# Smaller first loads at the head of a gated S5 + GELU-MLP kernel: first x slab alone, first weight slab in halves, one small load on another queue

## The chip, the cores and the metric

One core of a Trainium2 chip. The metric is the device time of one execution in microseconds (us). Runs repeat within about half a per cent for this kernel, so I give medians, ranges and the fastest runs, not only one time. "Ratio" is the mean time of one kernel's runs over the mean of the other's runs in the same rounds, so it is not quite the ratio of the medians that stand beside it.

## The reference, cut to what matters

Two branches over the same x (2048 tokens, 640 features), mixed by a gate:

```python
g = sigmoid((x * gate_w).sum(-1, keepdims=True))
a = S5(x)                      # x @ B_bar, a complex linear recurrence over time, @ C, + x * Dskip
b = gelu(x @ w1 + b1) @ w2 + b2        # w1: 640 x 1728
out = g * a + (1 - g) * b
```

Only the start of `x @ w1` matters here. The kernel contracts over 640 features in five steps of 128, called k=0 to k=4. For each step it needs a 128-feature slab of x, transposed, and a slab of W1 (128 x 1024, 256 KB).

## The kernel before: the parts that the change touches

The kernel gives each engine an ordered list of operations; priorities and assumed durations decide the order when the program is built, and semaphores carry the dependencies. In the profile's lines PE is TensorE, DVE VectorE, ACT ScalarE, POOL GpSimd and SP SyncE; SPq and ACTq are the queues from which these two issue loads, and a bank is one of the eight parts PS[0] to PS[7] of the memory that TensorE writes. For the first 512 tokens, slabs 0 and 1 of x are loaded plainly and transposed on TensorE; slabs 2 to 4 are loaded by transposing DMAs. All these loads are issued by SyncE, one after the other:

```python
KN = 2
load("xna", "sp", "l_xna", xn[0][:, :, 0:KN * 128], x2[0:512, 0:KN * 128]..., ["xna"], 0, ...)
w1load(0, "sp", 1)                       # W1 slab 0, 256 KB
w1load(1, "sp", 1.3)
xtrans(0, range(KN, KN + 1), 1.6, 0.8)   # x slab 2, transposing DMA
w1load(2, "sp", 2)
xtrans(0, range(KN + 1, KD), 3, 1.3)     # x slabs 3 and 4, transposing DMA
w1load(3, "sp", 4)
w1load(4, "sp", 5)
# ... then W1's remaining columns, B_re, B_im, the other x tiles, W2, C ...
load("b1b", "pool", "l_b1b", rows[RT:RT + 1, :]..., ["b1b"], prio=-50, ...)   # a one-row bias, twice

for n in (512,) * 6 + (256,):            # warm-up matmuls on constants
    nc.tensor.matmul(PS[4][:, 0:n], one..., one..., start=True, stop=True)

# 8 transposes: x slab 0 in banks 7 and 6, x slab 1 in banks 5 and 7; DVE copies them to xT
# first W1 matmuls: for k in 0..4, for jf in 0..7:  PS[jf] += W1[k, jf].T @ xT[k]
#   (k=0, jf=0 and 1 come in halves of 256 columns; k=0, jf=7, whose bank the transposes use, comes after k=1, jf=6)
```

## Time and profile before

| | before |
|---|---|
| time, median of the first 3 runs | 213.44 us (212.94 to 213.54) |
| profiled run | 212.76 us, span 211.5 us |
| first W1 matmul | 4.57 us |
| first matmul of the next stage (B) | 18.66 us |

The two lines below are the page's part on the chain that ended last: what each step back from the last instruction waited for.

```profile
PE 98%; issue 0%; DVE 0%
PE ps L772 27%; PE ps L642 22%; PE ps L821 21%; PE ps L685 20%; PE ps L622 4%; PE ps L400 1%; PE ps L786 1%; PE ps L663 1%; PE ps L412 0%; DVE osb L855 0%; PE ps L431 0%
```

The chain is TensorE from end to end; no DMA stands in it. Only what delays TensorE counts.

The same chain in order of time, its first 11.5 us (start, length, what):

```profile
0.78 2.93 PE ps L400 x7
3.71 1.03 PE ps L412 x8
4.74 2.38 PE ps L622 x13
7.12 0.06 PE ps L431
7.17 4.32 PE ps L622 x20
```

L400 is the warm-up, L412 the transposes, L622 the first W1 matmuls, L431 a small transpose of bias and parameter rows. The timeline of SyncE, which issues the loads (start, length of the issue, what):

```profile
0.74 0.45 SPq L326 DMA_DIRECT2D xn<-in_A_x_dram  x1
1.25 0.96 SPq L326 DMA_DIRECT2D W1sb<-in_B_w_dram  x2
2.26 1.20 SPq L333 DMA_TRANSPOSE xT<-in_A_x_dram  x1
3.51 0.59 SPq L326 DMA_DIRECT2D W1sb<-in_B_w_dram  x1
4.15 1.28 SPq L333 DMA_TRANSPOSE xT<-in_A_x_dram  x1
5.47 2.10 SPq L326 DMA_DIRECT2D W1sb<-in_B_w_dram  x4
```

An issue costs SyncE 0.42 to 0.59 us for a plain load and 1.2 to 1.3 us for a transposing one. The fourth line is W1 slab 2, the first of the last four is slab 3.

### The profile page before, as it was taken

The numbers are of one execution on the slowest core, as the hardware profiler recorded it, in microseconds if no ns is written. First come the engines' busy times: TensorE is split into PE (matmuls) and PEld (weight loads), VectorE is DVE, ScalarE is ACT, GpSimd is POOL, SyncE is SP. The second block draws the span as 40 slices with busy tenths as digits, with TensorE's granted clock in tenths as the row PEclk, the third lists the DMA queues.
The fourth block names the chain that finished last, engine by engine and source line by source line (L and its number), as shares of the span: only waits on it lengthen the run. The fifth ranks groups of instructions, "written<-read, shape, count | busy, mean of one in ns | idle before, by whom it ended". The sixth has DMA issues, their size and how long they took to land.

```text
span 211.5 us, 3140 instructions
## 1 busy us (share of the span) xinstructions
PE 208.1 (98%) x1266; PEld 121.2 (57%) x1276; DVE 189.3 (90%) x264; ACT 111.3 (53%) x201; POOL 3.0 (1%) x11
## 2 busy tenths in 40 slices
PE   8999999999999999999999999999999999999996
PEld 4444444444567776444466777544446777767775
DVE  2599999999999999999999969899999999899444
ACT  2588556678904334556953333456792444723330
POOL 2000000000000010000000001000000000000000
PEclk9999999999999999999999999999999999999999
DMA  5999699999100013100000014100000000010011
GB/s 164 290 246 183 158 225 300 303 213 197 42 0 3 31 38 120 62 0 0 0 3 0 0 48 143 39 23 3 0 0 2 3 31 31 31 34 0 31 34 62
DMA packets 31350, 16.35 MB, mean 77 GB/s; under 512 B 23144, under 2 KB 30440, under 8 KB 31336
## 3 DMA queue, kind: packets, MB, share of 16 engines
q1 hardware_dynamic: 30960, 14.83, 28.5%
q0 software_dynamic: 320, 1.31, 2.0%
q8 instruction: 10, 0.16, 0.3%
q14 instruction: 4, 0.03, 0.1%
q10 hardware_dynamic: 56, 0.01, 0.0%
HBM read 7.63 MB, written 2.62 MB: 48 GB/s over the span
## 4 chain that ended last, share of the span: by engine, by line
PE 98%; issue 0%; DVE 0%
PE ps L772 27%; PE ps L642 22%; PE ps L821 21%; PE ps L685 20%; PE ps L622 4%; PE ps L400 1%; PE ps L786 1%; PE ps L663 1%; PE ps L412 0%; DVE osb L855 0%; PE ps L431 0%
## 5 line engine op out<-in xcount | busy, mean ns | idle before, releaser
L772 PE MATMUL ps<-W2sb,Gl 128*128 128x320 bf16 x416 | 59.2, 299 | 0.0
L772 PEld LDWEIGHTS ps<-W2sb,Gl 128*128 128x128 bf16 x416 | 40.4, 98 | 17.1 <-issue 1.1
L642 PE MATMUL ps<-xT,W1sb 128*128 128x512 bf16 x215 | 47.5, 379 | 0.3
L821 PE MATMUL ps<-CT,H 128*128 128x320 bf16 (+2 forms) x330 | 45.5, 295 | 0.0
L725 DVE TENSOR_TENSOR_SCAN W<-atab,V 128x1280 bf16<-128x1280 f32 x16 | 44.3, 2811 | 0.3
L685 PE MATMUL ps<-xT,BT 128*128 128x512 bf16 x196 | 43.1, 379 | 0.3 <-issue 0.2
L821 PEld LDWEIGHTS ps<-CT,H 128*128 128x128 bf16 x330 | 31.9, 98 | 11.7
L800 ACT ACTIVATE E<-ps,g1col 128x320 bf16<-128x320 f32 x32 | 16.3, 526 | 39.7 <-PE ps L772 25.6
L642 PEld LDWEIGHTS ps<-xT,W1sb 128*128 128x128 bf16 x220 | 21.5, 98 | 26.0
L649 ACT ACTIVATE Gl<-ps,cols 128x512 bf16<-128x512 f32 x44 | 29.6, 688 | 10.0 <-PE ps L642 10.0
L685 PEld LDWEIGHTS ps<-xT,BT 128*128 128x128 bf16 x200 | 19.4, 98 | 23.5 <-ACT Gt L671 0.4
L694 ACT ACTIVATE U<-ps 128x512 bf16<-128x512 f32 x40 | 23.8, 597 | 15.0 <-PE ps L685 14.9
L832 ACT ACTIVATE E<-ps,gcol 128x320 bf16<-128x320 f32 x30 | 15.8, 527 | 22.6 <-PE ps L821 22.6
L759 ACT ACTIVATE ps<-b2b 128x320 f32<-128x320 bf16 x32 | 14.1, 441 | 1.1
L481 DVE TENSOR_TENSOR osb<-xg,E 128x640 bf16<-128x640 bf16 x15 | 7.3, 487 | 7.9 <-ACT E L832 7.6
L842 DVE SCALAR_TENSOR_TENSOR xg<-xn,gcol,dsk 128x640 bf16<-128x640 bf16 x16 | 13.9, 882 | 0.4
L597 DVE SCALAR_TENSOR_TENSOR scr<-xn,gwb 128x640 bf16<-128x640 bf16 x16 | 13.2, 822 | 0.4
L481 DVE TENSOR_TENSOR H<-H,V 128x1280 bf16<-128x1280 bf16 x16 | 12.5, 821 | 0.3
L481 DVE TENSOR_TENSOR V<-V,W 128x1280 bf16<-128x1280 bf16 x16 | 12.5, 821 | 0.3
L481 DVE TENSOR_TENSOR V<-mr,U 128x2560 bf16<-128x2560 bf16 x8 | 11.9, 1488 | 0.2
L481 DVE TENSOR_TENSOR H<-c,W 128x2560 bf16<-128x2560 bf16 x8 | 11.9, 1488 | 0.2
L481 DVE TENSOR_TENSOR W<-mi,U 128x2560 bf16<-128x2560 bf16 x8 | 11.9, 1483 | 0.0
(80 smaller groups left out, 99.9 us busy)
## 6 DMA issues: line engine op xcount, KB each, us to landing
out_dram<-osb SPq DMA_DIRECT2D x15, 160.0 KB, 1.8
W2sb<-in_B_w_dram SPq DMA_DIRECT2D x1, 2080.0 KB, 8.9
W1sb<-in_B_w_dram SPq DMA_DIRECT2D x5, 256.0 KB, 3.9
xn<-in_A_x_dram POOLq DMA_DIRECT2D x2, 640.0 KB, 4.6
xn<-in_A_x_dram SPq DMA_DIRECT2D x1, 640.0 KB, 7.9
W1sb<-in_B_w_dram SPq DMA_DIRECT2D x1, 480.0 KB, 5.8
W1sb<-in_B_w_dram SPq DMA_DIRECT2D x1, 400.0 KB, 6.5
xn<-in_A_x_dram SPq DMA_DIRECT2D x1, 384.0 KB, 6.0
```

The lines of the kernel that those rows point to most:

```text
L481: return inc("dve", nc.vector.tensor_tensor(out=o, in0=a, in1=b, op=o_))
L642: t = nc.tensor.matmul(PS[bank][:, :], W1sb[:, k, jf * 128:(jf + 1) * 128], xT[q][:, k, :], start=(k == 0), stop=(k == KD - 1))
L649: return inc("act", nc.scalar.activation(Gl[q % 2][:, jf, :], PS[bank][:, :], ACT.Gelu_apprx_tanh, bias=b1col[:, jf:jf + 1]))
L685: t = nc.tensor.matmul(PS[bank][:, :], BT[:, ci, kd, k * 128:(k + 1) * 128], xT[q][:, kd, :], start=(kd == 0), stop=(kd == KD - 1))
L694: return inc("act", nc.scalar.activation(dst, src, ACT.Copy, scale=1.0 if ci == 0 else -1.0))
L725: t = inc("dve", nc.vector.tensor_tensor_scan(out=g[:, ci, :], data0=a, data1=v[:, ci, :], initial=0.0, op0=ALU.mult, op1=ALU.add))
L759: return inc("act", nc.scalar.activation(PS[bank][:, 0:HALF], b2b[:, cols], ACT.Copy))
L772: t = nc.tensor.matmul(PS[bank][:, 0:HALF], Gl[q % 2][:, jf, t4 * 128:(t4 + 1) * 128], W2sb[:, jf, cols], start=False, stop=False, skip_gr ...
L800: return inc("act", nc.scalar.activation(E1[c % NE][:, cols], PS[bank][:, 0:HALF], ACT.Copy, scale=g1col[:, c:c + 1]))
L821: t = nc.tensor.matmul(PS[bank][:, 0:n], H[b % NHB][:, ci, k, s * 128:(s + 1) * 128], CT[:, ci, k, cols], start=(i == 0), stop=(i == 2 * K ...
L832: return inc("act", nc.scalar.activation(E2[c % NE][:, cols], PS[bank][:, 0:HALF], ACT.Copy, scale=gcol[:, c:c + 1]))
L842: return inc("dve", nc.vector.scalar_tensor_tensor(out=xg[c % 2][:, :], in0=xn[q % 2][:, c % 4, :], scalar=gcol[:, c:c + 1], in1=dsk[:, :] ...
```

## The change

Its intent is to start the first W1 matmuls earlier: a smaller first x slab lands sooner, half of W1's first slab is enough for half of the k=0 matmuls, the second x slab is transposed while k=0 already runs, and one warm-up matmul becomes superfluous. The diff, cut to its core:

```diff
-        load("xna", "sp", "l_xna", xn[0][:, :, 0:KN * 128], ..., ["xna"], 0, dur=0.45, lat=2.0)
-        w1load(0, "sp", 1)
+        for k in range(KN):
+            load(f"xna{k}", "sp", f"l_xna{k}", xn[0][:, :, k * 128:(k + 1) * 128], ...,
+                 [("xna", k)], (0, 1.2)[k], dur=0.45, lat=(2.0, 2.6)[k])
+        for h in range(2):
+            f0, f1 = h * FW // 2, (h + 1) * FW // 2
+            load(f"w1_0{h}", "sp", f"l_w10{h}", W1sb[:, 0, f0:f1], B_w1[0:128, f0:f1], [("w1", 0, h)], prio=1 + 0.1 * h, lat=2.6)
 ...
-        load("b1b", "pool", "l_b1b", ..., ["b1b"], prio=-50, dur=1.0)
+        load("b1b", "act", "l_b1b", ..., ["b1b"], prio=-101, dur=1.2)
 ...
-            for n in (512,) * 6 + (256,):
+            for n in (512,) * 5 + (256,):
 ...
-  op(f"xt{i}", ..., ["xna", "ident"], ..., prio=(-990, -989, -988, 2.5)[i])
+  op(f"xt{i}", ..., [("xna", k), "ident"], ..., prio=(-990, -989, 6.4, 6.5)[i])
+        def f_fill():                      # one filler matmul of 192 columns
+            return inc("pe", nc.tensor.matmul(PS[4][:, 0:192], one..., one..., start=True, stop=True))
+        op("fill", "pe", 0.2, (), [("bank", 4)], f_fill, prio=-980)
 ... (dependencies follow the new names)
```

SyncE's order becomes: x slab 0, W1 slab 0 first half, second half, x slab 1, W1 slab 1, and then as before. That is two issues more ahead of everything else.

More of the change, by code (lines that the diff above doesn't have):

```diff
@@ L353, in bass_gated_mix__ssm_conv_s5__dense_activation_gelu__prompt_kernel @@
         KN = 2
-        load("xna", "sp", "l_xna", xn[0][:, :, 0:KN * 128], x2[0:512, 0:KN * 128].rearrange("(c p) d -> p c d", p=128), ["xna"], 0, dur=0.45, lat=2.0)
-        w1load(0, "sp", 1)
+        for k in range(KN):
+            load(f"xna{k}", "sp", f"l_xna{k}", xn[0][:, :, k * 128:(k + 1) * 128], x2[0:512, k * 128:(k + 1) * 128].rearrange("(c p) d -> p c d", p=128),
+                 [("xna", k)], (0, 1.2)[k], dur=0.45, lat=(2.0, 2.6)[k])
+        for h in range(2):
+            f0, f1 = h * FW // 2, (h + 1) * FW // 2
+            load(f"w1_0{h}", "sp", f"l_w10{h}", W1sb[:, 0, f0:f1], B_w1[0:128, f0:f1], [("w1", 0, h)], prio=1 + 0.1 * h, lat=2.6)
         w1load(1, "sp", 1.3)
@@ L376, in bass_gated_mix__ssm_conv_s5__dense_activation_gelu__prompt_kernel @@
             load(nm, "act", "l_" + nm, rows[r0:r0 + src.shape[0], :], src, [nm], prio=-100 + i, dur=0.4)
-        load("b1b", "pool", "l_b1b", rows[RT:RT + 1, :].rearrange("o (a p) -> o a p", a=2),
-             B_b1[nmain:F].rearrange("(o p) -> o p", o=1).unsqueeze(1).broadcast_to([1, 2, FL]), ["b1b"], prio=-50, dur=1.0)
+        load("b1b", "act", "l_b1b", rows[RT:RT + 1, :].rearrange("o (a p) -> o a p", a=2),
+             B_b1[nmain:F].rearrange("(o p) -> o p", o=1).unsqueeze(1).broadcast_to([1, 2, FL]), ["b1b"], prio=-101, dur=1.2)
         def f_iota():
@@ L413, in f_xt @@
                 return inc("pe", t)
-            op(f"xt{i}", "pe", 0.11 * (c1 - c0), ["xna", "ident"], [("bank", bank)], f_xt, prio=(-990, -989, -988, 2.5)[i])
+            op(f"xt{i}", "pe", 0.11 * (c1 - c0), [("xna", k), "ident"], [("bank", bank)], f_xt, prio=(-990, -989, 6.4, 6.5)[i])
             def f_xc(k=k, pt=pt, c0=c0, c1=c1):
@@ L420, in bass_gated_mix__ssm_conv_s5__dense_activation_gelu__prompt_kernel @@
             op(f"xc{i}", "dve", 0.42, [("bank", bank)], [("xT", 0, k, c0)], f_xc, prio=-2000 + i)
+        def f_fill():
+            return inc("pe", nc.tensor.matmul(PS[4][:, 0:192], one.broadcast_to([128, 128]), one.broadcast_to([128, 192]), start=True, stop=True))
+        op("fill", "pe", 0.2, (), [("bank", 4)], f_fill, prio=-980)
         XK0 = [[("xT", 0, k)] for k in range(KD)]
@@ L569, in bass_gated_mix__ssm_conv_s5__dense_activation_gelu__prompt_kernel @@
         load("xnb", "sp", "l_xnb", xn[0][:, :, KN * 128:D], x2[0:512, KN * 128:D].rearrange("(c p) d -> p c d", p=128),
-             [("xn", 0, 0), ("xn", 0, 1)], 32.4, dur=1.0, lat=6.0, reads=["xna"])
+             [("xn", 0, 0), ("xn", 0, 1)], 32.4, dur=1.0, lat=6.0, reads=[("xna", k) for k in range(KN)])
         load("w2a", "sp", "l_w2a", W2sb[:, 0:NF - 1, :], B_w2[0:nmain, :].rearrange("(j p) d -> p j d", p=128), ["w2a"], prio=33, lat=8.0)
@@ L623, in f_mm @@
                                                       start=(k == 0 and t0 == 0), stop=(k == KD - 1), skip_group_check=jf < 2))
-                op(f"m1_0_{jf}_{k}_{t0}", "pe", d_mm(t1 - t0), (XK0[k] if h is None else XK0[k][h:h + 1]) + [("w1", k)], [("bank", jf)],
+                op(f"m1_0_{jf}_{k}_{t0}", "pe", d_mm(t1 - t0), (XK0[k] if h is None else XK0[k][h:h + 1]) + ([("w1", k)] if k else [("w1", 0, jf // (NW // 2))]), [("bank", jf)],
                    f_mm, prio=pe_prio())
@@ L644, in f_mm @@
                     return inc("pe", t)
-                op(f"m1_{q}_{jf}", "pe", KD * d_mm(512), XT[q] + ([("w1", k) for k in range(KD)] if jf < NW else [("w1", "r", int(jf * 128 >= FM))]), [("bank", bank)], f_mm, prio=pe_prio())
+                op(f"m1_{q}_{jf}", "pe", KD * d_mm(512), XT[q] + ([("w1", k) for k in range(1, KD)] + [("w1", 0, 0), ("w1", 0, 1)] if jf < NW else [("w1", "r", int(jf * 128 >= FM))]), [("bank", bank)], f_mm, prio=pe_prio())
                 def f_ge(jf=jf, bank=bank):
```

## The prediction

> **What bounds the kernel now.** TensorE. The chain of work that ended last is 98% PE, and matmul starts are back to back (0.216 us per 128x512) from the first W1 matmul at 4.57 us to 209.5 us of the 211.5 us span. So only the head can change, and passes one to one to the end.
>
> The head before (timeline): warm-up matmuls 0.78 to 3.50 us at 0.427 us each, half speed; the x slabs (256 KB, issued 0.74) land 3.63; eight transposes 3.67 to 4.57 (six of them 0.107 us apart: still half clock); then W1. The granted clock is recorded as full from 4.39 us. The Trainium skill ("TensorE: Matmul & The Clock Gate", Part 1) says the clock is released after about 3.4 us of sustained activity in a free-running window; 0.78 to 4.39 agrees. Work started earlier runs at half clock until then.
>
> **What the change does.**
> - Removes one 512-wide warm-up (0.43 us), adds one 192-wide filler (0.16 us cold); four of eight transposes move behind the clock release (4 x 0.05 us saved).
> - The x slab of k=0 is 128 KB in 512 packets of 256 B instead of 512 B. Packet times in the trace are 27 ns at 512 B and 18 ns at 256 B, so about 0.29 us less over 16 engines (estimate): landing 3.35 to 3.5. First copy to xT then ends near 4.1 to 4.2 (0.72 us after the transpose starts, as before), first W1 matmul about 4.15 instead of 4.57. W1's first half (issue about 1.25) should land by about 4.0.
> - The second slab's transposes come in the middle of k=0, and W1 matmuls behind them need their copies: transpose to copied is 0.6 us, with only one 0.22 us matmul between. Estimate: 0.2 us stall before (k=0, jf=5) and k=1. Start of k=1: 6.1 to 6.2, against 6.09 before. Most of the head gain is given back.
> - SyncE issues two more DMAs ahead of the rest, 0.42 to 0.49 us each. Later loads are issued about 0.9 us later. From 4.5 us on the DMA engines were fully busy, so part is absorbed; estimate: landings 0.5 us later. Slack before (landing against first use): W1 slab 2 0.85 us, slab 3 0.36 us, slab 4 1.3 us, W1 remainder 0.95 us, B_re 1.5 us. Slab 3 becomes tight: a stall of 0 to 0.4 us at k=3 (about 9.9 us).
> - The bias row's load moves from POOL (landed 4.65) to ACT; its reader at 6.95 has slack. Nothing.
>
> **Sum.** Head about 0 (-0.3 to +0.2), slab stall about +0.1 (0 to +0.5): nearly zero. Predicted 213.4 us against 213.44, range 212.7 to 214.2. Faster by over 2%: 0.01; within 2%: 0.98; slower: 0.01.
>
> **What would show it.** Right: first x landing near 3.4; first W1 matmul near 4.1 to 4.2; first transposing load issued near 3.2 instead of 2.26; holes of 0.1 to 0.3 us in PE around 5.5 to 6.2; a wait on W1 slab 3 near 10 us; after 13 us all shifted alike, by under 0.5 us. Wrong: the x slab landing at 3.6 or later, or W1 slabs landing a full 0.9 us later (stall at k=3 of 0.5 us).
>
> **What would make it wrong.** The clock release coming a window later because PE idles between the shorter warm-up and the slab: up to +1.7 us. Or late issues wholly absorbed and the k=0 slab landing near 3.1: down to -0.5 us.

## The result, and the profile after

| | before | after |
|---|---|---|
| time, median of 6 runs | 213.19 us (212.88 to 213.89) | 213.81 us (213.73 to 214.12) |
| ratio | | 1.0028, 95% interval 1.0009 to 1.0048 |
| profiled run, span | 211.5 us | 212.4 us |
| first x load lands | 3.63 us | 3.02 us |
| first W1 matmul | 4.57 us | 4.21 us |
| first matmul of k=1 | 6.09 us | 6.68 us |
| W1 slabs 2, 3, 4 land | 7.24, 9.45, 10.21 us | 8.72, 10.51, 12.44 us |
| first matmul of the B stage | 18.66 us | 19.62 us |

Within 2%, and a little slower. From the first B matmul to the end the two profiled runs take 192.79 and 192.81 us: the whole difference lies in the head. The first W1 matmul does come 0.36 us earlier, and k=1 already starts 0.59 us later. The chain that ended last, on the page after:

```profile
PE 93%; SPq 3%; DMA 2%; issue 1%; DVE 0%
PE ps L781 27%; PE ps L651 22%; PE ps L830 20%; PE ps L694 20%; DMA W1sb<-in_B_w_dram 2%; SPq L326 2%; PE ps L795 1%; SPq L333 1%; PE ps L672 1%; PE ps L631 1%; DVE osb L864 0%
```

A DMA and SyncE are in the chain now. The 2% and the two SPq shares are small, but they replace all of TensorE's work of the first 12 us. In order of time, from 3.52 us on, up to 20 us (pieces under 0.1 us left out; before 3.52 us it is SyncE's issues):

```profile
3.52 1.20 SPq L333
4.77 0.58 SPq L326
5.40 1.25 SPq L333
6.69 0.58 SPq L326
7.31 5.13 DMA W1sb<-in_B_w_dram
12.49 1.90 PE ps L631 x8
14.39 5.40 PE ps L651 x25
```

Read it from the bottom: the k=4 matmuls (12.49) waited for W1 slab 4 (issued at 7.31), and that for SyncE's queue of issues. The chain skips the transposes, the copies and the first four k steps: what TensorE won at 4 us no longer shows in it. Before, this stretch of the chain was TensorE alone. The margin is small, though: TensorE waited only 0.12 us for slab 4, so its own lateness, in the ledger below, is nearly as long a path in this profile. SyncE's issues after:

```profile
0.74 0.45 SPq L326 DMA_DIRECT2D xn<-in_A_x_dram  x1
1.25 1.15 SPq L326 DMA_DIRECT2D W1sb<-in_B_w_dram  x2
2.44 0.43 SPq L326 DMA_DIRECT2D xn<-in_A_x_dram  x1
2.92 0.56 SPq L326 DMA_DIRECT2D W1sb<-in_B_w_dram  x1
3.52 1.20 SPq L333 DMA_TRANSPOSE xT<-in_A_x_dram  x1
4.77 0.58 SPq L326 DMA_DIRECT2D W1sb<-in_B_w_dram  x1
5.40 1.25 SPq L333 DMA_TRANSPOSE xT<-in_A_x_dram  x1
6.69 2.10 SPq L326 DMA_DIRECT2D W1sb<-in_B_w_dram  x4
```

The first transposing load is issued at 3.52 instead of 2.26 us, 1.26 us later. And TensorE's timeline (in brackets the idle time before a piece, and what ended it), first before, where the W1 matmuls run on without a wait, then after:

```profile
4.57 2.54 PE L622 MATMUL ps<-xT,W1sb 128*128 128x256 bf16 x13
7.01 4.26 PE L622 MATMUL ps<-xT,W1sb 128*128 128x512 bf16 x19
```

```profile
3.08 0.63 PE L416 MATMUL ps<-ident,xn 128*128 128x128 bf16 x4
3.51 0.36 PE L427 MATMUL ps<-const-bfloat16-1.0 128*128 128x192 bf16 x1
4.21 1.74 PE L631 MATMUL ps<-xT,W1sb 128*128 128x256 bf16 x7 [0.34 <-DMA W1sb<-in_B_w_dram]
5.79 0.39 PE L416 MATMUL ps<-ident,xn 128*128 128x128 bf16 x4
6.01 1.69 PE L631 MATMUL ps<-xT,W1sb 128*128 128x512 bf16 x6
```

In the changed kernel L416 are the transposes, L427 is the filler and L631 the first W1 matmuls. The first W1 matmul waits for W1's first half (landed 4.08), not for the copy of x, which ended at 3.83.

The ledger of this profile, after against before, from the start times of single matmuls in the trace (us): first W1 matmul -0.36; the four 256-wide pieces took 0.81 instead of 0.44 us, because the clock's record turns full at 5.26 instead of 4.39 us, +0.37; the next matmul also, +0.12; four transposes now behind the first W1 matmul, +0.22; a hole before (k=0, jf=5), which waits for the second slab's copy, +0.22; waits at k=2, k=3 and k=4 for W1 slabs 2, 3 and 4: 0.18, 0.06 and 0.12. The sum is +0.93; the first B matmul came 0.96 us later.

Two suspects are mixed in this ledger, the late loads and the late release of the clock:

- **Theory A, late loads.** The two added issues (and what slows them) push back every later load. Where TensorE gets to k=2..4 sooner, it waits longer there. The end of the head is set by the landing of slabs 2 to 4.
- **Theory B, the clock.** With a warm-up matmul less and a hole of about 0.5 us before the first W1 matmul, the clock is released later. The Trainium skill ("TensorE: Matmul & The Clock Gate", Part 1, "What's actually happening") says that the activity window is free-running, so a third possibility is chance.

### The profile page after: what moved, and what is told of

It is laid out like the page before. It is cut to its first block, busy times and chain, and to the rows that moved or that the text cites. A ratio compares the mean times of both kernels' runs of the same rounds, so it can differ in the third digit from the quotient of the medians.

```text
span 212.4 us, 3144 instructions
## 1 busy us (share of the span) xinstructions
PE 208.5 (98%) x1266; PEld 121.1 (57%) x1276; DVE 189.4 (89%) x264; ACT 111.3 (52%) x201; POOL 2.5 (1%) x10
## 3 DMA queue, kind: packets, MB, share of 16 engines
q0 software_dynamic: 288, 1.31, 2.1%
## 4 chain that ended last, share of the span: by engine, by line
PE 93%; SPq 3%; DMA 2%; issue 1%; DVE 0%
PE ps L781 27%; PE ps L651 22%; PE ps L830 20%; PE ps L694 20%; DMA W1sb<-in_B_w_dram 2%; SPq L326 2%; PE ps L795 1%; SPq L333 1%; PE ps L672 1%; PE ps L631 1%; DVE osb L864 0%
## 5 line engine op out<-in xcount | busy, mean ns | idle before, releaser
L490 DVE TENSOR_TENSOR V<-s,W 128x2560 bf16<-128x2560 bf16 x8 | 11.9, 1485 | 0.0
```

The costliest lines, as they stand in the source:

```text
L490: return inc("dve", nc.vector.tensor_tensor(out=o, in0=a, in1=b, op=o_))
```

## The experiments

Times of all runs, grouped by the rounds that they shared with the kernel before. "Release" is when 512-wide matmuls change from 0.427 to 0.216 us apart in the profiled run (from the clock's record where there is one). "k=3 ready" is when the last k=2 matmul left TensorE free; "slab 3" is the landing of W1 slab 3; all in us of the profiled run.

```
kernel                     median   lowest..highest   ratio [95%]              release  k=3 ready  slab 3  k=3 starts  profiled time
before (50 runs)           213.14   212.75..213.92                              4.39      9.81      9.45     9.81        212.76
after                      213.81   213.73..214.12    1.0028 [1.0009 1.0048]    5.26     10.59     10.51    10.65        213.75
e1_bias_pool               213.81   213.38..213.99    1.0029 [1.0011 1.0047]    4.29     10.04     10.65    10.78        213.76
e2_bias_act                213.37   213.12..215.76    1.0036 [0.9997 1.0074]   ~5.2      10.15      9.44    10.15        213.12
e3_fill_long               214.03   213.96..214.08    1.0044 [1.0028 1.0061]   ~6.6      11.11     10.85    11.11        214.08
e4_w1_whole                215.26   213.40..215.84    1.0085 [1.0048 1.0122]    9.65     12.71     10.51    12.71        215.72
e5_x1_act                  213.90   213.17..215.23    1.0043 [1.0017 1.0070]   ~6.0      10.67      9.78    10.67        213.68
e6_w1_halves (5 runs)      213.24   213.01..213.36    1.0006 [0.9990 1.0022]    3.73     10.12      9.86    10.12        213.12
e7_whole_fill              213.77   213.54..214.19    1.0032 [1.0014 1.0050]    5.57     10.91     10.00    10.91        213.94
e8_late_issue              213.54   213.17..214.07    1.0021 [1.0004 1.0039]    4.76     10.01     10.90    11.03        214.07
e9_slabs_act (5 fast)      214.78   213.79..215.16    1.0063 [1.0037 1.0088]     (a new wait stands earlier, see below)
e10_slabs_bank             214.92   214.19..215.93    1.0080 [1.0053 1.0108]     (the same)
e11_before_slabs_act       214.35   213.66..215.08    1.0039 [1.0014 1.0064]     (the same)
e12_bank4                  212.94   212.76..213.39    0.9984 [0.9964 1.0005]    4.87      9.92      9.67     9.92        212.88
```

For the eleven rows that have a start of k=3, the profiled time less that start lies between 202.95 and 203.10 us. So the start of k=3 is the whole story to within 0.15 us, and it is the later of two things: TensorE being ready, and slab 3 having landed (where TensorE waited, it began 0.13 to 0.14 us after the landing).

### 1. The bias load back on POOL

```diff
-        load("b1b", "act", ..., ["b1b"], prio=-101, dur=1.2)
+        load("b1b", "pool", ..., ["b1b"], prio=-50, dur=1.0)
```

> The changed kernel with the bias row's load back on POOL. Theory A (late loads): what the changed kernel loses is set by W1 slab 4, which landed at 12.44 us and was waited for; the bias load took 1.18 us to issue on ACT and held up SyncE's issues beside it, so the first transposing load should be issued near 3.2 us instead of 3.52, slab 4 land about 0.3 us earlier, and the time fall by 0.1 to 0.3 us (ratio to before about 1.001 to 1.002). Theory B (clock release late, 5.26 us instead of 4.39, because PE idled from 3.7 to 4.2): no change, ratio 1.0028.

The time did not move (1.0029 against 1.0028 of before), though the fastest runs did (213.38 against 213.73). SyncE's first transposing load was issued at 3.34 instead of 3.52 us; so the bias load cost the other queue about 0.2 us. The profile is the most telling of all, because in it the clock was released early, at 4.29 us. (The hole before the first W1 matmul was also shorter, 0.22 instead of 0.55 us, as W1's first half landed at 3.82 instead of 4.08; so this profile alone doesn't show that the early release is chance.) TensorE's timeline, with its wait in brackets:

```profile
7.24 2.97 PE L631 MATMUL ps<-xT,W1sb 128*128 128x512 bf16 x13
10.78 0.59 PE L631 MATMUL ps<-xT,W1sb 128*128 128x512 bf16 x2 [0.58 <-DMA W1sb<-in_B_w_dram]
```

TensorE was ready for k=3 at 10.04 us, half a microsecond before the changed kernel's run, and then waited for slab 3 until 10.78. The time is the same, 213.76 against 213.75. An earlier release of the clock is taken back in full by the loads: theory A for this run. Part of A's expectation failed: the time did not fall by the earlier issue, since slab 3 landed no earlier (10.65 against 10.51). Slab 4, which the expectation named, did land 1.17 us earlier (11.27), and was not waited for. The profile shows one more wait: TensorE was ready for k=1 at 6.09 us and began at 6.32, 0.14 us after W1 slab 1 had landed (6.18; before: 5.73).

### 2. The bias load alone, in the kernel before

```diff
-        load("b1b", "pool", ..., ["b1b"], prio=-50, dur=1.0)
+        load("b1b", "act", ..., ["b1b"], prio=-101, dur=1.2)
```

> The kernel before with only the bias row's load moved to the head of the ACT queue. Theory A: SyncE's issues come up to 0.3 us later, W1 slab 3 had 0.36 us of slack, so the time stays within 0.1 us of before (ratio 0.9995 to 1.001). If the bias load by itself were the cost of the change: +0.3 us or more, ratio over 1.0015.

The load's issue took 1.19 us of ACT's queue, as in the changed kernel (ACT timeline, here and below it the first load of before):

```profile
0.97 1.19 ACTq L326 DMA_DIRECT2D rows<-in_B_b_dram  x1
```

```profile
0.97 0.56 ACTq L326 DMA_DIRECT2D rows<-in_A_Lambda_re_dram  x1
```

SyncE's two W1 issues beside it took 1.15 instead of 0.96 us and the first transposing load came 0.19 us later. There was no wait for slab 3. The ratio, 1.0036, rests on one run of 215.76, and the interval holds 1; the median is 0.4 us above before. Inconclusive as to time: a small cost of this move is possible, and none was shown. The single long run is unexplained.

### 3. A filler that covers the hole

```diff
-  nc.tensor.matmul(PS[4][:, 0:192], ...)
+  for n in (512, 320):
+      nc.tensor.matmul(PS[4][:, 0:n], ...)
```

> The changed kernel with a filler of 512 and 320 columns instead of 192, which covers the PE hole of 3.7 to 4.2 us. Theory B: the clock is released near 4.4 us again and the time falls by about 0.4 us (ratio 1.001). Theory A: the release may come earlier, but PE then waits longer for W1 slabs 2 to 4, which still land at 8.7, 10.5 and 12.4 us: no gain, ratio 1.0025 to 1.003. A third theory, that the release is free-running and has nothing to do with the hole: release anywhere, and no gain.

It was slower than the changed kernel, not faster, and its profile released the clock at about 6.6 us although TensorE had no hole longer than about 0.1 us from 0.78 us on until then. So theory B, that the 0.5 us hole is what makes the release late, fails: without the hole the release came later still in the profile, and none of the six runs was faster than 213.96. In this profile no load was waited for at k=3; the half clock alone made TensorE late. Why its six runs agree within 0.12 us is not shown by one profile.

### 4. W1's first slab whole, and 7. the same with the hole filled

```diff
-        for h in range(2): load(f"w1_0{h}", "sp", ..., W1sb[:, 0, f0:f1], ...)
+        load("w1_0", "sp", ..., W1sb[:, 0, 0:FW], ..., [("w1", 0, 0), ("w1", 0, 1)], prio=1, lat=2.6)
```

> The changed kernel with W1's first slab loaded whole: one DMA issue less in front of the rest. Theory A: later loads are issued about 0.5 us earlier, slab 4 lands 0.4 to 0.5 us earlier (near 12.0) and the time falls by 0.3 to 0.4 us (ratio about 1.001), although the first W1 matmul starts later, near 4.4 instead of 4.2. Theory B: no gain, since the hole before the first W1 matmul gets longer; ratio 1.003 or more.

Run 7 adds this to it:

```diff
-  nc.tensor.matmul(PS[4][:, 0:192], ...)
+  for n in (512, 512, 512, 64):
+      nc.tensor.matmul(PS[4][:, 0:n], ...)
```

> The run with W1's first slab whole (213.4 to 215.8 us, clock released at 9.65 us in its profile) with a filler of 1600 columns that covers its PE hole of 3.7 to 4.96 us. If the hole makes the clock gate miss a window: no run over 214.6, median near 213.8, release before 7.7 us. If the late release is chance alone: the same spread, up to 215.8.

Run 4, TensorE's timeline; then run 7:

```profile
3.52 0.37 PE L425 MATMUL ps<-const-bfloat16-1.0 128*128 128x192 bf16 x1
4.96 1.87 PE L629 MATMUL ps<-xT,W1sb 128*128 128x256 bf16 x6 [1.06 <-DMA W1sb<-in_B_w_dram]
6.62 0.63 PE L414 MATMUL ps<-ident,xn 128*128 128x128 bf16 x4
7.04 2.97 PE L629 MATMUL ps<-xT,W1sb 128*128 128x512 bf16 x7
```

```profile
3.52 1.54 PE L427 MATMUL ps<-const-bfloat16-1.0 128*128 128x512 bf16 x4
4.87 1.37 PE L632 MATMUL ps<-xT,W1sb 128*128 128x256 bf16 x6
6.08 0.39 PE L414 MATMUL ps<-ident,xn 128*128 128x128 bf16 x4
6.30 1.91 PE L632 MATMUL ps<-xT,W1sb 128*128 128x512 bf16 x7
```

With the hole, seven W1 matmuls take 2.97 us from 7.04 on: still half clock, up to 9.65 us. Four of the six runs took 214.8 to 215.8 us, two 213.4 and 213.9. With useless work in the hole the six runs took 213.5 to 214.2, 1.5 us less in the median, though nothing useful was added. So a hole of this length (1.27 us between the filler's last column and the first W1 matmul) does make late releases likely; one of 0.5 us, as in the changed kernel, was not seen to in any of its six runs (none over 214.12). Run 5 below, with a hole of 0.60 us before its transposes, had one run of 215.23, which is unexplained. Run 4 also saved the second half's issue, 0.5 us. Slab 4, which the expectation of theory A named, landed at 11.74 instead of 12.44, as expected and more; slab 3 landed at 10.51, as in the changed kernel, and the late clock hides what the earlier loads are worth.

The traces allow one more check of the clock. Nine of them hold its record (before, after, runs 1, 4, 6, 7, 8, 10 and 12). The full clock lasts 208.21 us in eight and 204.80 us in run 4; these are 61 and 60 times their difference, 3.41 us. If the clock is therefore taken to change only on a grid of 3.41 us, placed differently in each execution, the changed kernel's release (5.26) could have come earlier only at 1.84 us, when matmuls had run for 1.1 us: its hole did not delay it. In run 4 the grid point before the release is 6.23, and the 3.41 us up to it held 1.31 us of idle TensorE, most of it the hole. The 3.41 us before the recorded releases held 0 to 0.69 us (most in run 6; worked out from matmul starts and column counts). This is a reading of one profile per kernel, not an experiment, but it agrees with runs 3, 4 and 7.

### 5. The second x slab from ACT

```diff
-  load(f"xna{k}", "sp", ..., (0, 1.2)[k], ...)
+  load(f"xna{k}", ("sp", "act")[k], ..., (0, -102)[k], ...)
   (with W1's first slab whole and the bias load on POOL)
```

> The changed kernel with the second x slab issued from ACT (head of its queue), W1's first slab whole and the bias row back on POOL, so that SyncE issues the later loads at the times of the kernel before (first transposing load near 2.26 us), while the 256 B packets of the two x slabs stay. If late issue is what the change costs: W1 slab 3 lands near 9.5 us, no wait at k=3, fastest runs at or below those of before (212.5 to 212.9), ratio 0.998 to 1.000. If the extra DMA work of short packets is what it costs: slab 3 lands near 10.2 or later and the fastest runs stay at 213.3 or more.

SyncE's later issues were back at the times of before (first transposing load at 2.27), and slab 3 landed at 9.78 us, 0.7 to 0.9 us earlier than in the changed kernel and run 1, 0.3 us later than before. TensorE never waited for it. So late issue is the larger part of the late landings, and the short packets at most the rest (a single landing is no better than a few tenths of a us, see run 8; in run 12, whose loads are those of before, slab 3 landed at 9.67). But the time did not fall: both x slabs now moved at once, and slab 0 landed at 3.63 instead of 3.02 us, just as the undivided load of before; the first W1 matmul came at 4.75 and the release at about 6.0 us.

### 6. The halves alone, in the kernel before

```diff
-        w1load(0, "sp", 1)
+        for h in range(2): load(f"w1_0{h}", "sp", ..., W1sb[:, 0, f0:f1], ..., prio=1 + 0.1 * h, ...)
```

> The kernel before with only W1's first slab in halves: one more DMA issue on SyncE, no short packets, the x slabs as before. Late issue: the first transposing load is issued near 2.75 us, slab 3 lands about 0.4 us later (near 9.9), which its 0.36 us of slack nearly covers: fastest runs 212.8 to 213.1. Short packets as the cause: no change at all, 212.8.

As expected of late issue: the first transposing load at 2.78, slab 3 at 9.86 us. The fastest run is 213.01 (before 212.75 in the same rounds), the ratio 1.0006 with 1 in its interval. In the profile the cost was at W1 slab 1 (landed 6.27, k=1 begun at 6.40 us, 0.31 us after TensorE was ready).

### 8. The issue delay alone, in the kernel before

```diff
         w1load(0, "sp", 1)
+        for i in range(2):     # two loads of 1.2 KB into a tile that nobody reads
+            load(f"junk{i}", "sp", f"l_junk{i}", junk[i * 16:i * 16 + 5, :], A_log_dt..., prio=1.1 + 0.1 * i)
         w1load(1, "sp", 1.3)
```

> The kernel before with two tiny DMAs (1.2 KB each, into a tile that nobody reads) issued by SyncE between W1 slabs 0 and 1: the issue delay of the change alone, without its bytes, packets, halves or transposes. Late issue as the cause: first transposing load near 3.2 us, slab 3 lands near 10.3, a wait at k=3 of about 0.5 us, fastest runs 213.2 to 213.6, and the spread between runs shrinks as in the changed kernel. Short packets or the move of the transposes as the cause: 212.8 as before.

This is the test of theory A without anything else of the change. The two small issues delayed slab 3's issue by 0.63 us only. TensorE's timeline:

```profile
7.20 2.97 PE L625 MATMUL ps<-xT,W1sb 128*128 128x512 bf16 x13
11.03 2.32 PE L625 MATMUL ps<-xT,W1sb 128*128 128x512 bf16 x9 [0.86 <-DMA W1sb<-in_B_w_dram]
```

and the chain that ended last, from 2.92 us on to the k=3 matmuls (pieces under 0.15 us left out), with SyncE's issues and a slab as in the changed kernel (there it is slab 4, here slab 3):

```profile
2.92 1.21 SPq L333
4.18 0.57 SPq L326
4.79 1.26 SPq L333
6.09 4.80 DMA W1sb<-in_B_w_dram
11.03 1.67 PE ps L625 x7
```

Slab 3 landed 1.45 us later than before, TensorE waited 1.02 us longer than its matmul spacing, and the ratio, 1.0021 (1.0004 to 1.0039), is most of the change's 1.0028, though the intervals overlap. Two issues in the wrong place are enough for a loss that is clear of the noise. The profiled run is the slowest of the six (214.07; median 213.54), so a wait of 1.02 us is the upper end and not typical. The landing slipped by more than the issue did, and I have no experiment for why; single landings scatter (slab 3, issued at 6.69 and 6.71 us in the changed kernel and run 3, landed at 10.51 and 10.85; issued at 6.17 and 6.24 in runs 4 and 7, at 10.51 and 10.00); the DMA engines' share in the stretch from 3 to 10.5 us was about as high in both kernels. That the spread between the runs would shrink was not borne out here (213.17 to 214.07).

### 9, 10 and 11. W1 slabs 2 and 3 from ACT

```diff
-        w1load(2, "sp", 2)
+        w1load(2, "act", -90)       # behind ACT's small row loads
-        w1load(3, "sp", 4)
+        w1load(3, "act", -89)
```

Run 9 is the changed kernel with this and the bias load on POOL; run 10 also puts the second slab's transposes into one bank, so that no k=0 matmul waits for their copy; run 11 is the kernel before with the two slabs moved and nothing else.

> The changed kernel (bias row on POOL) with W1 slabs 2 and 3 issued from ACT behind its small row loads, so that SyncE's two long transposing issues no longer stand in front of them: issued near 2.6 and 3.1 us instead of 4.8 and 6.7. If the change's own head gain is real and only hidden by the late slab 3: no wait at k=3, slab 3 landing before 9.6 us, fastest runs 212.3 to 212.7, below those of before (212.75), and the spread that the clock's release gives comes back. If the second slab's traffic just takes the DMA engines from the loads that stand earlier (W1 slab 1, the transposing loads), a new wait shows at k=1 or k=2 and the time stays at 213.2 or more.

> The same with the second x slab's four transposes in bank 7 alone and one copy, so that no matmul of k=0 waits for that copy. If the hole of 0.22 us near 6.2 us in the changed kernel costs its length once the loads are no longer late: 0.1 to 0.25 us less than the run without it (fastest runs 212.1 to 212.6).

> Control: the kernel before with W1 slabs 2 and 3 issued from ACT and nothing else. Slab 3 had 0.36 us of slack in its profile and the head (x landing 3.6, transposes, copies) set its fastest runs, so the fastest stay at 212.7 to 212.9 and the ratio at 0.999 to 1.001. If earlier slabs by themselves gain, it falls below 212.6.

All three were slower, 0.8 to 1.4 us above before in the same rounds (medians). The waits of TensorE from 4 to 13 us (us in total, times, longest), run 9 and then run 11:

```profile
PE ps L416 <- DMA xn<-in_A_x_dram: 1.0, 1, 1.0
PE ps L631 <- DMA W1sb<-in_B_w_dram: 0.8, 1, 0.8
```

```profile
PE ps L622 <- DMA W1sb<-in_B_w_dram: 1.2, 1, 1.2
PE ps L622 <- DMA xT<-in_A_x_dram: 0.2, 1, 0.2
```

Slabs 2 and 3 were issued at 2.6 and 3.0 us and did land early in run 9 (6.05 and 8.11), but what TensorE needs first paid for it: x slab 1 landed at 6.22 instead of 4.71 (run 1), W1 slab 1 at 7.94 instead of 6.18. In run 11 slab 1 landed at 7.85 instead of 5.73 us. This agrees with the Trainium skill ("Trainium Kernel Development and Optimization", Key Constraints), which says that issuing from several queues shares the same 16 DMA engines and saves issue time only, and with "DMA: Bandwidth & Descriptors" (Queues, rings and completion order), which says that an engine goes round between the queues it has work for. In one queue the order of issue is also an order of urgency; a second queue takes that away. Whether the 0.22 us hole of the changed kernel costs anything could not be told, since run 10 waited for W1 slab 1 in its place. One run of run 9 (217.31) is slow and is in neither its ratio nor its row of the table.

### 12. A version that might beat both

```diff
-            bank = (7, 6, 5, 7)[i]
+            bank = (7, 6, 5, 4)[i]
-            op(f"xt{i}", "pe", ..., prio=(-990, -989, -988, 2.5)[i])
+            op(f"xt{i}", "pe", ..., prio=(-990, -989, -988, -987)[i])
```

> A small attempt to beat both: the kernel before, with the last transpose pair in bank 4 instead of bank 7, so that it need not wait 0.16 us for bank 7's copy; no load moves. If the head sets the fastest runs of before, and W1 slab 3's 0.36 us of slack covers the gain: first W1 matmul near 4.45 instead of 4.57, fastest runs 212.6 to 212.7 instead of 212.75, ratio 0.999 to 1.000, too small to be clear of the clock's spread. If the loads set them: no change at all.

The kernel before, with its last transpose pair in a bank of its own (the new priority keeps the pair where it was, ahead of W1), starts W1 at 4.50 us in its profile instead of 4.57. The median was 212.94 against 213.38 in the same rounds and the ratio 0.9984 (0.9964 to 1.0005): not clear of the noise. The fastest runs stayed at 212.76. That would fit with the loads setting the fastest runs, against what I expected, but no profile shows it: in the profiled run (212.88) slab 3 was not waited for. I would keep it, as it costs nothing, and not claim it as a gain.

## Why the prediction was right or wrong, point by point

- **The bound and the class: right.** Only the head differs; the rest is 192.79 against 192.81 us. 213.81 us lies in the range 212.7 to 214.2 and within 2%. The centre, 213.4, foresaw no change; measured is +0.6 us. The prediction's own sign of being wrong, W1 slabs landing a full 0.9 us later, did come about, so that the time still lies in the range is owed to the range's width, and partly to luck.
- **The first slab: better than estimated.** It landed at 3.02 us, not 3.35 to 3.5, and between 3.06 and 3.15 in runs 1, 3, 4, 7, 9 and 10. The estimate of 0.29 us from packet times missed 0.3 us; the first use was still near 4.2 us, but W1's first half set it (landed 4.08), not the copy.
- **The hole before (k=0, jf=5): right.** 0.2 us predicted, 0.22 us in the profile.
- **The start of k=1: wrong in this profile, near in another.** 6.1 to 6.2 predicted, 6.68 measured where the clock was released at 5.26, 6.32 in run 1 where it was released at 4.29. I had taken the release of one profile as a fixed time. It lay between 3.73 and about 6.6 us in the runs without a long hole. And the list of slacks left out W1 slab 1, which had 0.36 us before (landed 5.73, used at 6.09), as little as slab 3: in run 1 TensorE was ready at 6.09, as predicted, and waited for it.
- **"Later loads are issued about 0.9 us later": too small.** 1.26 us; about 0.2 of that is the bias load on ACT, of which I had said "Nothing" (0.18 us less with it on POOL, 0.19 us more with it alone).
- **"Estimate: landings 0.5 us later": the step that failed.** Slabs 2, 3 and 4 landed 1.48, 1.06 and 2.23 us later. That is why the +0.1 us for "slab stall" was too small: with an early clock TensorE waited 0.74 us at k=3 (run 1), and the issue delay alone brought 1.02 us in run 8's profile.
- **"Head about 0 (-0.3 to +0.2)", added to the stall: wrong in size and in kind.** At k=1 the head was 0.59 us late in the profile, and 0.23 in run 1, there by W1 slab 1. And head and loads don't add; the later of the two decides. That is seen best in the changed kernel and run 1: k=3 ready at 10.59 and 10.04, k=3 begun at 10.65 and 10.78, time 213.75 and 213.76. It also fits that the changed kernel's six runs spread over 0.4 us and the six of before in the same rounds over 1.0 us, as the time of the clock's release shows only where no load is waited for; but run 8, which also waits for the slab, spread over 0.9 us, so that is argued, not shown.

Open: why landings slip by more than issues, the long run of experiment 2, how much the short packets cost by themselves (0.3 us of landing in run 5, within the scatter), and what the moved transposes and their hole cost (0.44 us in the ledger): no run has them without the late loads and with nothing else changed.

## What to carry to other kernels

Before an early load is split, count what stands behind it in the same queue: here each plain issue took about half a microsecond, and two of the loads behind it, W1 slab 1 (the next) and slab 3 (five issues further on), had only 0.36 us of slack. A gain at the front is kept only up to the slack of the next thing that the bound engine waits for; list landing against first use for each of them, and compare the two chains of waits, not the first timestamp. And where runs of one kernel differ by more than the effect, look for the event that moves (here the clock's release) before a difference of two profiles is read as an effect.

## What the Trainium skill lacked or had wrong

- "TensorE: Matmul & The Clock Gate", Part 1, says that the clock is released after at least one busy window of about 3.4 us. In run 6 it was released at 3.73 us, 2.95 us after the first matmul (0.78), so a window need not be filled by matmuls. The page lacks how much of a window must be busy: by the reading of the clock's records above, 0.69 us of idle time in it did not hold the release back (run 6), and 1.31 us did (run 4, released at 9.65 us). That the window is free-running, as the page says, agrees with releases from 3.73 to about 6.6 us without a long hole; but each kernel has one profile, so chance and kernel are not told apart.
- "DMA: Bandwidth & Descriptors" gives issue costs in sequencer cycles for a plain copy and a small transpose, but none in time for these shapes: a transposing load of 512 rows held SyncE for 1.20 us, and a broadcast one-row load of 0.2 KB held ACT's queue for 1.18 us where a five-row load took 0.56, and slowed the plain issues on SyncE beside it by 0.19 us.
- The same page says that transfers under 512 B are slower. Here a 256 B packet took 18 ns and a 512 B one 27 ns; halving the bytes with as many packets still brought the landing from 3.63 to 3.02 us. The page has no figure for such a load from SyncE: its measured table is for loads issued from GpSimd.
- None of the pages on DMA and TensorE says how a delay of issue passes to the landing under load; here 0.63 us became 1.45 us (run 8, one profile against one).
